# Dividing TensorE's step behind its sixth chunk in a one-core cached-attention kernel, with the maximum under a condition of its own

## The chip, the cores and the metric

The kernel runs on one core of a Trainium2 chip. The metric is the device time of one execution in microseconds (us). Three executions of the kernel before took 1268.61, 1270.12 and 1272.01 us; their median, 1270.12 us, is the time before. One more execution was profiled: 1268.6 us, of which the profile's span, from its first to its last instruction, is 1266.8 us.

## The reference

One token `x` of 448 numbers attends, with 16 query heads, to a cache of 8 key/value heads with 65,536 positions each, and the result is mixed with that of a small token mixer.

```python
q = (x @ wq)                                   # 16 heads of 256
k, v = repeat(k_cache, 2), repeat(v_cache, 2)  # each cached head serves 2 query heads
p = softmax(einsum("bhqd,bhkd->bhqk", q, k) * 256 ** -0.5)
a = einsum("bhqk,bhkd->bhqd", p, v).reshape(1, 1, 4096) @ wo
b = mixer(x)                                   # layernorm, 1792 features, gelu, back to 448
g = sigmoid((x * gate_w).sum(-1))
return g * a + (1 - g) * b
```

Keys and values are bf16, 268 MB each, and every one is used once.

## The kernel before, in words

The keys of the 8 heads are cut into `NP` = 32 *pairs* of 16,384 positions (4 to a head, `PPH`), numbered 0 to 31 here. A pair has `BODY` = 8 *chunks* of 2048 positions, 0 to 7. K and V of a pair are 8.4 MB each (`NV` = 128 rows of 64 KB).

**Transfers.** All large ones stand in SyncE's program, in one queue, in this order for pair j: K of pair j, when chunk 3 of pair j-1 has been transposed (`sem_tr`); then V of pair j-1, when the products of the probabilities and V of pair j-2 are done (`sem_pv`); with a head's first pair also its rows of `wo`, when the head before has been projected (`s_proj`). K lies in a ring of one and a half pairs (`kring`), V in one buffer (`vbuf`). The order was written out by hand; pairs 2, 3 and 31 have K in two halves. V of the last pair comes in five pieces (`pieces`): rows 0 to 47 go to the ring when pair 30 is transposed; 48 to 95, 96 to 111, 112 to 123 and 124 to 127 go to `vbuf` when the products of pair 30 are done (`sem_pv` at 31). Behind them come the two halves of the last head's `wo` (`sem_wl`).

**A chunk.** `transposes(k)` (L348) turns 16 tiles of 128x128 f32 words, four to each of four PSUM banks. VectorE (L681) copies two banks to SBUF and ScalarE (L821) the two others. `scores(k)` (L369) are 32 small matmuls against `qcur`, the two query columns of the head; they need the copies. Written T0 to T7 and S0 to S7 below.

**A pair's end.** `maxima` (L390, L392): VectorE reduces the scores to a running maximum per head (L687), TensorE transposes and spreads it, VectorE forms the negative maximum and the fading factor, ScalarE the exponentials `pT` (L808), and VectorE fades the accumulator `acc` (up to L710).

**Values.** `values(v)` adds pair v-1's part to `acc`: eight matmuls for the denominators (L397), then 128 matmuls with V's rows (L404); the wait for V stands between the two. For the last pair the first 48 rows are done in `first_of_last`, right behind the maximum, rows 48 to 111 in `values(32)`, and the last 16 in `tail` with the roles of the operands exchanged (L445), behind two matmuls that bring `acc` to the other layout (L452); then the last projection (L471) and the output.

**TensorE's loop** has 35 passes. Registers count the pairs: `k_reg` for `keys`, `l_reg` for `last_keys`, `v_reg` for `values`. In a steady pass it does, for pair j: `keys` (T0, then T1 S0 up to T6 S5), `values` of pair j-1, `last_keys` (T7 S6 S7), then, in a new head, the projection of the old one, for 14 pairs four matmuls of the mixer, then `maxima`. Of the first passes some hold only a part: `values` of pair 0 comes in a pass of its own before any keys of pair 1, and that of pair 1 before those of pair 2 (`cap_reg`, `LEAD` = 2). At the end, pass 33 holds `keys` of pair 31, `values` of pair 30, `last_keys` and `maxima` of pair 31 and `first_of_last`; pass 34 holds `values(32)` and `tail`. Before T0 of a head TensorE waits on `s_qc` for VectorE's copy of the head's queries to `qcur` (L767, behind the maximum, and where there is one the mixer step, of the head's last pair).

## Time and profile before

| what | us |
|---|---|
| three runs | 1268.61, 1270.12, 1272.01 |
| profiled execution | 1268.6 |
| its span | 1266.8 |
| TensorE matmuls busy | 922.7 |
| TensorE weight loads busy | 867.2 |
| ScalarE busy | 544.0 |
| VectorE busy | 497.1 |
| transposes L348, 4096 of them | 555.5 |
| values L404, 4032 of them | 122.1 |
| scores L369, 8192 of them | 236.7 |

The transfers move 544.22 MB in that span, 430 GB/s on average. Busy times of engines overlap each other, so they do not add up to the span; what matters is which engine or queue the others wait for at each place, and that is read from the chain of waits and the timeline.

### The profile page before, as it was taken

The numbers are of one execution on the slowest core, as the hardware profiler recorded it, in microseconds if no ns is written. First come the engines' busy times: TensorE is split into PE (matmuls) and PEld (weight loads), VectorE is DVE, ScalarE is ACT, GpSimd is POOL, SyncE is SP. The second block draws the span as 40 slices with busy tenths as digits, with TensorE's granted clock in tenths as the row PEclk, the third lists the DMA queues.
The fourth block names the chain that finished last, engine by engine and source line by source line (L and its number), as shares of the span: only waits on it lengthen the run. The fifth ranks groups of instructions, "written<-read, shape, count | busy, mean of one in ns | idle before, by whom it ended". The sixth has DMA issues, their size and how long they took to land.

```text
span 1266.8 us, 40261 instructions
## 1 busy us (share of the span) xinstructions
PE 922.7 (73%) x17201; PEld 867.2 (68%) x17201; DVE 497.1 (39%) x1125; ACT 544.0 (43%) x692; POOL 0.9 (0%) x7
## 2 busy tenths in 40 slices
PE   4588877678676687766887667876669766688685
PEld 3577866578676687665777566875668766687684
DVE  3233444343443444544445333333334332343341
ACT  2354543344433454443544334443444443354451
POOL 0000000000000000000000000000000000000000
PEclk9798887789777898778888789877789877898787
DMA  9999999999999999999999999999999999999998
GB/s 416 432 396 430 447 430 430 441 435 430 430 430 443 432 430 430 430 443 432 430 430 436 437 432 430 430 437 437 432 430 430 437 435 435 430 430 430 427 434 346
DMA packets 12054, 544.37 MB, mean 430 GB/s; under 512 B 1417, under 2 KB 1676, under 8 KB 2956
## 3 DMA queue, kind: packets, MB, share of 16 engines
q1 hardware_dynamic: 11954, 544.22, 99.6%
q8 instruction: 7, 0.11, 0.0%
q10 hardware_dynamic: 90, 0.01, 0.0%
q14 instruction: 3, 0.02, 0.0%
HBM read 544.22 MB, written 0.00 MB: 430 GB/s over the span
## 4 chain that ended last, share of the span: by engine, by line
DMA 68%; PE 30%; issue 1%; DVE 0%; SPq 0%; DVEq 0%
DMA kring<-in_A_k_cache_dram 65%; PE kst L348 24%; PE sps L369 5%; DMA vbuf<-in_A_v_cache_dram 3%; PE acc L404 2%; PE acc L397 0%; PE sps L392 0%; DVE mcol L687 0%; PE sps L445 0%; PE sps L452 0%; DVE acc L710 0%; PE sps L390 0%; DVE mrow L692 0%; DVE accs L715 0%; DVE mdiag L694 0%
## 5 line engine op out<-in xcount | busy, mean ns | idle before, releaser
L348 PE MATMUL kst<-ident,kring 128*128 128x128 f32 x4096 | 555.5, 296 | 266.8 <-DMA kring<-in_A_k_cache_dram 233.5
L821 ACT ACTIVATE ktT<-kst 128x1024 bf16<-128x1024 bf16 x512 | 498.5, 1021 | 539.9 <-PE kst L348 539.5
L348 PEld LDWEIGHTS kst<-ident,kring 128*128 128x128 f32 x4096 | 504.7, 154 | 281.3 <-issue 280.6
L681 DVE COPY ktT<-kst 128x1024 bf16<-128x1024 bf16 x512 | 354.2, 692 | 636.0 <-PE kst L348 612.1
L369 PEld LDWEIGHTS sps<-qcur,ktT 128*128 128x128 bf16 x8192 | 238.1, 96 | 2.6
L369 PE MATMUL sps<-qcur,ktT 128*128 128x2 bf16 x8192 | 236.7, 163 | 0.0
L404 PE MATMUL acc<-vbuf,pT 128*2 128x256 bf16 x4032 | 122.1, 282 | 5.9 <-DMA vbuf<-in_A_v_cache_dram 5.6
L404 PEld LDWEIGHTS acc<-vbuf,pT 128*2 128x2 bf16 x4032 | 94.3, 86 | 25.5 <-DMA vbuf<-in_A_v_cache_dram 5.7
L804 ACT ACTIVATE fade<-mdif 128x2 f32<-128x2 f32 x32 | 6.5, 203 | 112.0 <-DVE mdif L698 112.0
L392 PEld LDWEIGHTS sps<-mdiag,mones 2*128 2x128 f32 x64 | 13.0, 252 | 28.4 <-DVE mdiag L694 28.4
L392 PE MATMUL sps<-mdiag,mones 2*128 2x2 f32 x64 | 15.8, 313 | 21.3 <-DVE mdiag L694 21.3
L808 ACT ACTIVATE pT<-sps,mneg 128x64 f32 x128 | 30.4, 334 | 0.0
L826 ACT ACTIVATE z_b<-z_b 128x448 bf16<-128x448 bf16 x14 | 8.1, 576 | 48.1 <-DVE z_b L668 48.1
L687 DVE TENSOR_REDUCE mcol<-sps 128x2 f32<-128x256 f32 x32 | 13.5, 422 | 33.6 <-PE sps L369 33.6
L390 PE MATMUL sps<-ident,mcol 128*2 128x128 f32 x32 | 9.7, 302 | 12.9 <-DVE mcol L690 10.5
L397 PE MATMUL acc<-pT,ones_sq 128*128 128x32 bf16 x256 | 11.7, 179 | 7.7 <-DVE acc L710 3.4
L710 DVE TENSOR_SCALAR acc<-acc,fader 128x256 f32<-128x256 f32 x32 | 15.8, 493 | 2.5
L397 PEld LDWEIGHTS acc<-pT,ones_sq 128*128 128x128 bf16 x256 | 8.6, 97 | 10.8 <-issue 7.2
L692 DVE TENSOR_REDUCE mrow<-sps 2x1 f32<-2x128 f32 x32 | 8.9, 279 | 15.9 <-PE sps L390 15.9
L390 PEld LDWEIGHTS sps<-ident,mcol 128*2 128x2 f32 x32 | 2.6, 80 | 16.2 <-DVE mcol L690 12.6
L697 DVE TENSOR_SCALAR mneg<-sps 128x2 f32<-128x2 f32 x32 | 5.1, 159 | 18.7 <-PE sps L392 18.7
L460 PEld LDWEIGHTS acc<-sel,accs 128*64 128x64 f32 x112 | 10.8, 214 | 0.9
(108 smaller groups left out, 163.4 us busy)
## 6 DMA issues: line engine op xcount, KB each, us to landing
kring<-in_A_k_cache_dram SPq DMA_DIRECT2D x8, 4096.0 KB, 24.3
wo_sb<-in_A_wo_dram SPq DMA_DIRECT2D x7, 448.0 KB, 28.6
vbuf<-in_A_wq_dram SPq DMA_DIRECT2D x1, 3072.0 KB, 10.3
kring<-in_A_v_cache_dram SPq DMA_DIRECT2D x1, 3072.0 KB, 38.8
vbuf<-in_A_v_cache_dram SPq DMA_DIRECT2D x1, 3072.0 KB, 9.6
vbuf<-in_A_v_cache_dram SPq DMA_DIRECT2D x1, 1024.0 KB, 11.6
vbuf<-in_A_v_cache_dram SPq DMA_DIRECT2D x1, 768.0 KB, 13.1
vbuf<-in_A_wq_dram SPq DMA_DIRECT2D x1, 512.0 KB, 11.1
```

The source lines that it names most:

```text
L348: ins = pe.transpose(kst[:, b, i * P:(i + 1) * P], kring_f[:, at + NT * (k % DC) + 4 * b + i, :], ident[:, :])
L369: ins = pe.matmul(sps[:, 0, 2 * (NT * k + nt):2 * (NT * k + nt) + 2], ktT[:, par, b, ntl * DH + dj:(ntl + 1) * DH:2], qcur[:, dj, :], star ...
L390: pe.transpose(mxT, mcol[:, :], ident[:, :]).then_inc(s_mT, 1)
L392: pe.matmul(mxB, mones[:, :], mdiag[:, :], start=True, stop=True).then_inc(s_mB, 1)
L397: pe.matmul(acc[:, DENC:SELC], ones_sq[:, :], pT[:, r, :], start=False, stop=(r == BODY - 1), skip_group_check=True)
L404: ins = pe.matmul(acc[o:o + REP, 0:DH], pT[:, r, 2 * nt:2 * nt + 2], buf[:, n, :], start=False, stop=False, skip_group_check=True)
L460: ins = pe.matmul(dst[hh * HP:(hh + 1) * HP, i:i + 1], accs[:, i:DH:2 * REP], sel[:, hh:hh + 1], start=False, stop=True, skip_group_check= ...
L681: vec.tensor_copy(ktT[:, k % KTB, b, :], kst_b[:, b, :]).then_inc(sem_ev[b], 1)
L687: vec.tensor_reduce(out=mcol[:, :], in_=scores_all.rearrange("p (n hh) -> p hh n", hh=REP), axis=AX.X, op=ALU.max)
L710: vec.tensor_scalar(acc[:, 0:DENC], acc[:, 0:DENC], fader[:, :], None, op0=ALU.mult).then_inc(s_acc, 1)
L808: ins = act.activation(pT[:, bass.ds(p0, DC), hh:2 * NT:REP], scores_all.rearrange("p (a r n hh) -> p a hh r n", a=2, r=DC, hh=REP)[:, hal ...
L821: act.activation(ktT[:, k % KTB, b, :], kst_b[:, b, :], AF.Copy).then_inc(sem_ev[b], 1)
```

## The change

`keys` ends behind its sixth chunk, and `last_keys` takes the rest. A pair is then T0, T1 S0 up to T5 S4 | `values` of the pair before | T6 S5 T7 S6 S7 | maximum. A constant `CUT` = 6 says where.

`maxima`, with what stood ahead of it (projection, mixer matmuls) and `first_of_last` behind it, leaves the branch of `last_keys` and gets a branch of its own with a register of its own, `m_reg`: it runs when `last_keys` of that pair is done and `values` of all pairs before it (`v_reg == m_reg`).

`values` gets a second condition. `need_reg` is 0 until `keys` of pair 31 is done and 32 from then on, and `values` runs only if `l_reg >= need_reg`. So pass 33 holds `keys` and `last_keys` of pair 31 and nothing else, pass 34 `values` of pair 30, then the maximum of pair 31 and `first_of_last`, and a pass 35 is added with `values(32)` and `tail`.

The semaphore `s_qc`, TensorE's wait for it and the registers that counted heads for it go. `done` holds `c + 1` once for the four banks of a chunk. SyncE's, VectorE's and ScalarE's programs stay as they were but for the increments of `s_qc`.

```diff
+    CUT = 6
 ...
+                done = pe.snap(c + 1, min_val=1, max_val=NC)
 ...
-                        pe.wait_ge(sem_ev[b], c + 1)
+                        pe.wait_ge(sem_ev[b], done)
 ...
             def keys(c0, j, *where):
-                for k in range(1, BODY - 1):
+                for k in range(1, CUT):
                     transposes(k, c0 + k, j, *where)
                     scores(k - 1, c0 + k - 1, j1)
             def last_keys(c0, x2):
-                transposes(BODY - 1, c0 + (BODY - 1), None, None, x2)
-                for k in range(BODY - 2, BODY):
-                    scores(k, c0 + k, None)
+                for k in range(CUT, BODY):
+                    transposes(k, c0 + k, None, None, x2)
+                    scores(k - 1, c0 + k - 1, None)
+                scores(BODY - 1, c0 + BODY - 1, None)
 ...
-            with nc.Fori(0, NP + LEAD + 1, 1, engines=on, head_slot={pe.engine: 0}):
+            with nc.Fori(0, NP + LEAD + 2, 1, engines=on, head_slot={pe.engine: 0}):
                 with pe.If(val(k_reg) < val(cap_reg)):
-                    with pe.If(val(mk_reg) == PPH):
-                        pe.reg_mov(mk_reg, 0)
-                        pe.reg_add(gk_reg, gk_reg, 1)
-                    pe.wait_ge(s_qc, pe.snap(gk_reg, min_val=1, max_val=H))
                     keys(...)
-                    pe.reg_add(mk_reg, mk_reg, 1)
-                with pe.If(val(v_reg) < val(l_reg)):
-                    ... values(v) ...
+                    with pe.If(val(k_reg) == NP):
+                        pe.reg_mov(need_reg, NP)
+                with pe.If(val(v_reg) < val(m_reg)):
+                    with pe.If(val(l_reg) >= val(need_reg)):
+                        ... values(v) ...
                 with pe.If(val(l_reg) < val(k_reg)):
                     last_keys(...)
-                    ... projection of a head, mixer matmuls ...
                     pe.reg_add(l_reg, l_reg, 1)
-                    maxima(pe.snap(l_reg, min_val=1, max_val=NP))
-                    with pe.If(val(l_reg) == NP):
-                        first_of_last()
+                with pe.If(val(m_reg) < val(l_reg)):
+                    with pe.If(val(v_reg) == val(m_reg)):
+                        ... projection of a head, mixer matmuls ...
+                        pe.reg_add(m_reg, m_reg, 1)
+                        maxima(pe.snap(m_reg, min_val=1, max_val=NP))
+                        with pe.If(val(m_reg) == NP):
+                            first_of_last()
                 with pe.If(val(v_reg) == NP):
                     tail()
 ...
-            vec.tensor_copy(qcur[:, :, :], qT[:, :, 0:REP]).then_inc(s_qc, 1)
+            vec.tensor_copy(qcur[:, :, :], qT[:, :, 0:REP])
```

More of the change, by code (lines that the diff above doesn't have):

```diff
@@ L66, in bass_gated_mix__gqa_block_cached__mixer_token_mlp__decode_kernel @@
     NLATE = 112
+    CUT = 6
+    assert DC < CUT < BODY
     NRING = 48
@@ L198, in bass_gated_mix__gqa_block_cached__mixer_token_mlp__decode_kernel @@
         sem_kc = [new_sem("sem_kc%d" % i) for i in range(3)]
-        s_qc = new_sem("s_qc")
         sem_v = new_sem("sem_v")
@@ L530, in _ @@
             cap_reg = reg("cap_reg", 1)
-            mk_reg = reg("mk_reg", 0)
-            gk_reg = reg("gk_reg", 1)
+            m_reg = reg("m_reg", 0)
+            need_reg = reg("need_reg", 0)
             mv_reg = reg("mv_reg", 0)
@@ L551, in _ @@
                     pe.reg_add(k_reg, k_reg, 1)
-                    pe.reg_add(mk_reg, mk_reg, 1)
-                with pe.If(val(v_reg) < val(l_reg)):
-                    pe.reg_add(v_reg, v_reg, 1)
-                    pe.reg_add(mv_reg, mv_reg, 1)
-                    pe.reg_add(cap_reg, v_reg, 1)
-                    v = pe.snap(v_reg, min_val=1, max_val=NP)
-                    values(v)
-                    with pe.If(v >= LEAD):
-                        pe.reg_mov(cap_reg, NP)
+                    with pe.If(val(k_reg) == NP):
+                        pe.reg_mov(need_reg, NP)
+                with pe.If(val(v_reg) < val(m_reg)):
+                    with pe.If(val(l_reg) >= val(need_reg)):
+                        pe.reg_add(v_reg, v_reg, 1)
+                        pe.reg_add(mv_reg, mv_reg, 1)
+                        pe.reg_add(cap_reg, v_reg, 1)
+                        v = pe.snap(v_reg, min_val=1, max_val=NP)
+                        values(v)
+                        with pe.If(v >= LEAD):
+                            pe.reg_mov(cap_reg, NP)
                 with pe.If(val(l_reg) < val(k_reg)):
@@ L564, in _ @@
                     pe.reg_sub(x2l_reg, NV, x2l_reg)
-                    with pe.If(val(mv_reg) == PPH):
-                        pe.reg_mov(mv_reg, 0)
-                        g1 = pe.snap(gv_reg, min_val=1, max_val=H)
-                        pe.wait_ge(s_cp, g1)
-                        clear(acc[:, 0:NACC])
-                        by_row(acc[:, SELC:NACC]).then_inc(s_sel, 1)
-                        pe.wait_ge(sem_wo, pe.snap(g1 * 16, min_val=16, max_val=16 * H))
-                        pe.wait_ge(s_oTn, g1)
-                        project(range(2 * REP)).then_inc(s_proj, 1)
-                        pe.reg_add(gv_reg, gv_reg, 1)
@@ L575, in _ @@
-                    with pe.If(l > MIX0):
-                        with pe.If(l < MIX0 + FT + 1):
-                            pe.wait_ge(s_pb, val(mix_reg, 1, FT))
-                            pe.reg_add(mix_reg, mix_reg, 1)
-                            for q in range(NCG):
-                                pe.matmul(prj[32 * q:32 * q + 1, WG:2 * WG], w2cur[:, :],
-                                          gu[:, q * WG:(q + 1) * WG], start=False, stop=True, skip_group_check=True)
-                    pe.reg_add(l_reg, l_reg, 1)
@@ L583, in _ @@
-                    maxima(pe.snap(l_reg, min_val=1, max_val=NP))
-                    with pe.If(val(l_reg) == NP):
-                        first_of_last()
+                    pe.reg_add(l_reg, l_reg, 1)
+                with pe.If(val(m_reg) < val(l_reg)):
+                    with pe.If(val(v_reg) == val(m_reg)):
+                        with pe.If(val(mv_reg) == PPH):
+                            pe.reg_mov(mv_reg, 0)
+                            g1 = pe.snap(gv_reg, min_val=1, max_val=H)
+                            pe.wait_ge(s_cp, g1)
+                            clear(acc[:, 0:NACC])
+                            by_row(acc[:, SELC:NACC]).then_inc(s_sel, 1)
+                            pe.wait_ge(sem_wo, pe.snap(g1 * 16, min_val=16, max_val=16 * H))
+                            pe.wait_ge(s_oTn, g1)
+                            project(range(2 * REP)).then_inc(s_proj, 1)
+                            pe.reg_add(gv_reg, gv_reg, 1)
+                        with pe.If(val(m_reg) > MIX0):
+                            with pe.If(val(m_reg) < MIX0 + FT + 1):
+                                pe.wait_ge(s_pb, val(mix_reg, 1, FT))
+                                pe.reg_add(mix_reg, mix_reg, 1)
+                                for q in range(NCG):
+                                    pe.matmul(prj[32 * q:32 * q + 1, WG:2 * WG], w2cur[:, :],
+                                              gu[:, q * WG:(q + 1) * WG], start=False, stop=True, skip_group_check=True)
+                        pe.reg_add(m_reg, m_reg, 1)
+                        maxima(pe.snap(m_reg, min_val=1, max_val=NP))
+                        with pe.If(val(m_reg) == NP):
+                            first_of_last()
@@ L767, in _ @@
                     vec.tensor_copy(qcur[:, :, :], qT[:, :, bass.ds(vec.snap(q_reg, min_val=REP, max_val=HQ - REP), REP)]
-                                    ).then_inc(s_qc, 1)
+                                    )
                     vec.reg_add(q_reg, q_reg, REP)
```

## The prediction

> **What bounds the kernel now.** I read the page first, then the waits, then the end of the timeline with the transfers beside it, then the start. The page:

> ```profile
> span 1266.8 us, 40261 instructions
> ...
> DMA  9999999999999999999999999999999999999998
> ...
> DMA 68%; PE 30%; issue 1%; DVE 0%; SPq 0%; DVEq 0%
> ```

> The transfer engines are busy in every slice, and waiting for them makes up 68% of the chain. One pair (400.0 to 438.7 us, asked for as a stretch) moves 434 GB/s at a DMA share of 1.00. In the waits of the whole run

> ```profile
> PE kst L348 <- DMA kring<-in_A_k_cache_dram: 233.5, 29, 10.5
> ...
> PE acc L404 <- DMA vbuf<-in_A_v_cache_dram: 5.6, 1, 5.6
> ```

> TensorE waits for K 29 times, 233.5/29 = 8.1 us each, and for V once: for that of pair 30. So steady pairs are set by bytes; only places where the queue runs dry can pay. The timeline's end shows one:

> ```profile
> 1235.82 0.36 PE L397 MATMUL acc<-pT,ones_sq 128*128 128x32 bf16 x8
> 1241.79 6.09 PE L404 MATMUL acc<-vbuf,pT 128*2 128x256 bf16 x128 [5.61 <-DMA vbuf<-in_A_v_cache_dram]
> 1247.94 1.85 SPq L265 DMA_DIRECT2D vbuf<-in_A_v_cache_dram  x4
> 1247.96 1.96 PE L348 MATMUL kst<-ident,kring 128*128 128x128 f32 x16
> 1249.75 1.74 PE L369 MATMUL sps<-qcur,ktT 128*128 128x2 bf16 x64
> 1249.84 0.95 SPq L314 DMA_DIRECT2D wo_sb<-in_A_wo_dram  x2
> 1252.25 0.27 PE L390 MATMUL sps<-ident,mcol 128*2 128x128 f32 x1 [0.76 <-DVE mcol L690]
> 1256.46 2.73 PE L404 MATMUL acc<-kring,pT 128*2 128x256 bf16 x48
> 1259.79 2.23 PE L404 MATMUL acc<-vbuf,pT 128*2 128x256 bf16 x64 [0.27 <-issue]
> 1264.27 0.37 PE L471 MATMUL prj<-wo_sb,oTn 128*1 128x112 bf16 x16 [0.25 <-DVE oTn L728]
> ```

> The last V pieces are requested only when pair 30's values end (1247.9). The transfers by issue give 9.6, 11.6, 13.1 and 13.3 us to landing for the four and 13.4 for the last `wo` half: landings at 1257.5, about 1260.0, 1261.9, 1262.6 and 1263.7. The piece ahead of them (requested 1210.25, 38.8 us) landed at 1249.0, and the DMA share falls to 0.18 in 1247.5 to 1248.5 and 0.48 in 1249.5 to 1250.5: a hole of about 1.1 us, since a request takes about 1 us to its first packets.

> **Steady pairs: cost at nothing, by cover.** Work is moved, not added: T6 (1.81) and S5 (0.78), 2.6 us, go behind `values`. In pair 10 T6 began at 423.12, and V, requested at 389.70 with 34.7 us to landing, came at 424.4. The eight denominator matmuls and their branch (0.6) now come first, so TensorE waits some 0.7 us for V (in other pairs 0 to 2), a wait this trace lacks. Behind it stand the 128 matmuls (3.66), T6 S5, T7 at about 430.7 instead of 429.9, the maximum, ScalarE's and VectorE's copies, and T0. The cover is the wait for K before T0: 9.87 us here, 5.58 in the tightest steady pair (T0 at 365.36). Were it gone, K's request would be late, but that has a second cover: K is requested at 416.70, 7.7 us before V ahead of it lands. V's request (429.98 before) now goes 0.8 us later or up to 1.7 earlier, with K in transfer until 443.8. Bounds: 0 below, since no byte moves sooner; above, each us beyond 5.6 + 7.7 costs 28 us in all. I take 0.

> **The clock** could eat cover. Two neighbouring 3.41 us stretches (columns: length, busy PE, PEld, DVE, ACT, POOL, granted clock, DMA, GB/s):

> ```profile
> 1209.27:1212.68 3.41, 2.66 (x74) 2.51 (x72) 1.71 (x4) 1.94 (x2) 0.00 (x0) 1.00 0.92 396
> 1212.68:1216.09 3.41, 1.32 (x6) 1.09 (x6) 1.79 (x9) 1.06 (x5) 0.00 (x0) 0.50 0.99 423
> ```

> **The removed wait on `s_qc`: nothing.** The copy to `qcur` ended at 164.8, T0 of the next head began at 170.41, on K. S0 still follows VectorE's copy of chunk 0, which follows that copy. Register work, and the added branches of each pass, lie in the same cover.

> **The end: the gain.** SyncE's order, and when V of pair 30 lands (1241.75), stay. T6 S5 T7 S6 S7 of pair 31 took until 1235.7 + 1.8 + 1.6 = 1239.1 with nothing between; pair 30's late V (landing 1202.97 against T6's 1201.47) shifts all by about 0.9, to 1240.0; then branches and the way round the loop (1.4 between the last L392 at 131.2 and T0 at 132.65, an upper bound: behind 64 queued scores part of it hides) and denominators 0.4. That is 1240.4 to 1241.8: `values` starts about when it did. Its first wait for V still stands ahead of everything of the end.

> Behind `values` the maximum follows at once. L390 stood 1252.25 - 1247.88 = 4.4 us behind it; now about 0.5. With the same later steps the 48 ring rows end at 1259.19 - 3.9 = 1255.3 instead of 1259.2, and the next V piece lands at 1257.5: 2.2 of the 3.9 become a wait for it. From there landings rule: 16 rows behind 1260.0 end at 1260.7; copy and L452 (1.1) 1261.9; L445 behind 1262.6, ending 1262.9; the projection's second half behind 1263.7, ending about 1263.95 instead of 1264.67. **Gain 0.7 us** with the requests where they were.

> Requests can come sooner: TensorE was idle 5.61 us before `values`, ran it at half clock and needed 6.09; pair 10 needed 3.66. Now the idle time is about 2, with 1.6 of scores ahead of it: between cold and warm. If `values` ends 1 us sooner the hole of 1.1 us closes, and all landings with it: gain 1.8 and no more, as bytes then follow without a gap. I take 1.2, nearer neither end, since the phase of the 3.41 us stretches is not fixed by the kernel. Sum: 1266.8 - 1.2 = 1265.6 span, 1267.4 with the 1.8 us around it. The profiled execution is 1.5 under the median, so 1270.1 - 1.2 = **1268.9 us**.

> **Rival 1, warm: 1268.3.** [...] The mechanism from rows: `values` at 3.66 ends at 1245.5, requests 2.4 sooner, hole closed, gain 1.8. For: after 1.90 us of idling ahead of 72.56 the clock stayed at 1.00. Against: the two stretches above, which fell without an idle one. Chance 0.2.

> **Rival 2, slower: 1272.9.** TensorE's instructions arrive in packets, seven in all and none after 66 us. Twice the first pass waited for one; a packet at 50.7 and one at 58.3 stand before these rows (waits in brackets):

> ```profile
> 53.60 3.67 PE L348 MATMUL kst<-ident,kring 128*128 128x128 f32 x16 [9.51 <-issue]
> ...
> 61.26 0.37 PE L390 MATMUL sps<-ident,mcol 128*2 128x128 f32 x1 [2.30 <-issue]
> ```

> T7 and L390 each started 2.9 us behind their packet. The seventh started at 65.4, so what it holds runs from 68.3. [...] Then `values` of pair 0 starts at about 69 and, mostly at half clock, ends at 74.7 instead of 70.7; V of pair 1 (requested 70.71, when K had all but landed at 72.4) goes 4.0 later, the queue stands empty, and all behind moves: 1270.1 - 1.2 + 4.0. The moved T6 S5 themselves cost nothing there: they run from 46.6, in the gap of 9.51. [...] Chance 0.18. [...]

> **Rival 3, `values` late: 1271.4.** If shift, branches and a cold pair 30 (3.4) add up, `values` of pair 30 starts after V's landing; each us then opens the hole by one. Say 2 us late and at 6.09: landings 2.0 later, less the 0.7 gained, +1.3 net. For: little slack (0 to 1.3). Against: starting late, it starts warm. Chance 0.07.

> **Rival 4, it gains nothing: 1270.1.** The bytes end where they did and `wo` hides the rest. Chance 0.05; the forecast keeps 0.5.

> **Numbers.** 0.3%, 3.8 us, is about what a measurement of this kernel can tell from no change; no case alone reaches it. Low end: 1.8 gained and the runs' spread below the median, 1.5: 1266.8. High end: rival 2 and half a us: 1273.4. Faster by over 0.3%: 0.07, from rival 1 and spread. Slower: 0.11, rival 2 or 3 with spread, and cover I misjudged. Same: 0.82.

> **Right or wrong.** Right: waits for V before L408 (L404 so far) in most pairs, up to 2 us; K's landings 38.7 apart; L394 (L390 so far) within a us of the end of pair 30's values; DMA share near 1 from 1242 to the last landing; the wait for the next V piece behind the ring rows. Wrong: first V request of pair 1 after 72 us; T0 late for K in steady pairs; values of pair 30 starting after 1242.

## The result and the profile after

The changed kernel took **1275.17 us** (median of 9 runs, 1273.02 to 1276.88), the kernel before 1270.31 us in runs beside it (9 runs, 1267.86 to 1272.18). The ratio is 1.0038 with a 95% interval of 1.0026 to 1.0050: slower by 4.9 us. The forecast was 1268.9 us with a range up to 1273.4; the result lies above the range. Rival 2 is what happened, in the profiled run at a higher price than it was given, and the end gained nothing. The profiled execution took 1276.85 us, its span 1274.6 us.

From the page of the changed kernel:

```profile
DMA  9979999999999999999999999999999999999998
...
DMA 62%; PE 33%; issue 3%; DVE 1%; SPq 0%; DVEq 0%; ACT 0%
```

Before, all slices but the last of the DMA row were 9. Now the third one, 64 to 96 us, is a 7. The chain has 3% "issue" instead of 1%. The damage is done in one place near the start. The timeline there (start, duration, engine, line, idle time before), first before the change and then after it:

```profile
64.60 0.40 PE L397 MATMUL acc<-pT,ones_sq 128*128 128x32 bf16 x8 [1.72 <-DVE acc L710]
...
64.92 5.74 PE L404 MATMUL acc<-vbuf,pT 128*2 128x256 bf16 x128
70.71 0.33 SPq L265 DMA_DIRECT2D vbuf<-in_A_v_cache_dram  x1
```

```profile
63.54 0.37 PE L394 MATMUL sps<-ident,mcol 128*2 128x128 f32 x1 [3.06 <-issue]
...
71.50 0.40 PE L401 MATMUL acc<-pT,ones_sq 128*128 128x32 bf16 x8 [6.34 <-issue]
71.83 6.03 PE L408 MATMUL acc<-vbuf,pT 128*2 128x256 bf16 x128
77.91 0.33 SPq L266 DMA_DIRECT2D vbuf<-in_A_v_cache_dram  x1
```

The denominators of pair 0 waited 6.34 us for "issue", that is for nothing that the profile shows. VectorE's fading of `acc`, which they need, was done at 66.74. TensorE's seventh instruction packet (the times of packets are those of the records of TensorE's instruction queue) began at 67.76. V of pair 1 was requested at 77.91; before, at 70.71. K of pair 1 had landed at 72.58 and nothing else was in the queue. The stretches, with the columns of the prediction's clock rows:

```profile
70.00:72.00 2.00, 0.50 (x14) 0.40 (x18) 0.00 (x0) 0.00 (x0) 0.00 (x0) 0.50 0.01 4
72.00:74.00 2.00, 2.00 (x44) 1.32 (x40) 0.00 (x0) 0.00 (x0) 0.00 (x0) 0.50 0.00 0
...
78.00:80.00 2.00, 0.64 (x6) 0.64 (x7) 0.00 (x0) 0.00 (x0) 0.00 (x0) 1.00 1.57 524
```

From 70 on to behind 78 the queue moved next to nothing, for 8 us. V of pair 1 landed at 99.69 (before 92.67, so +7.02) and V of pair 30 at 1248.76 (before 1241.75, +7.01): what was lost at the start is carried through 29 pairs without a change. The end, from the timeline of TensorE and SyncE:

```profile
1242.19 1.96 PE L351 MATMUL kst<-ident,kring 128*128 128x128 f32 x16 [1.20 <-issue]
...
1246.57 1.74 PE L372 MATMUL sps<-qcur,ktT 128*128 128x2 bf16 x64
1250.77 0.38 PE L401 MATMUL acc<-pT,ones_sq 128*128 128x32 bf16 x8 [2.46 <-issue]
1251.08 5.22 PE L408 MATMUL acc<-vbuf,pT 128*2 128x256 bf16 x128
1256.35 1.80 SPq L266 DMA_DIRECT2D vbuf<-in_A_v_cache_dram  x4
1257.60 0.27 PE L394 MATMUL sps<-ident,mcol 128*2 128x128 f32 x1 [1.30 <-issue]
...
1266.01 1.48 PE L408 MATMUL acc<-vbuf,pT 128*2 128x256 bf16 x48 [0.74 <-DMA vbuf<-in_A_v_cache_dram]
1268.48 0.61 PE L408 MATMUL acc<-vbuf,pT 128*2 128x256 bf16 x16 [0.99 <-DMA vbuf<-in_A_v_cache_dram]
```

`values` of pair 30 no longer waits for V. It starts 2.3 us behind V's landing (1251.08 against 1248.76), so the last requests come 7.59 us behind that landing instead of 6.19, and the last landing is 23.32 us behind it instead of 21.95. From the last landing to the end it is 2.55 us instead of 3.10. Together, V of pair 30 to the end: 25.87 instead of 25.05, +0.82. So the profiled difference of 7.8 us is 7.0 at the start, nothing between and 0.8 at the end. The 0.8 alone shows little, since profiles with the same order of the end differ by more (below, under the end in the account of the prediction).

### The profile page after: what moved, and what is told of

The parts are those of the page before. It is cut to its first block, busy times and chain, and to the rows that moved or that the text cites. A ratio compares the mean times of both kernels' runs of the same rounds, so it can differ in the third digit from the quotient of the medians.

```text
span 1274.6 us, 40489 instructions
## 1 busy us (share of the span) xinstructions
PE 939.0 (74%) x17201; PEld 878.3 (69%) x17201; DVE 496.7 (39%) x1125; ACT 544.9 (43%) x692; POOL 0.9 (0%) x7
## 4 chain that ended last, share of the span: by engine, by line
DMA 62%; PE 33%; issue 3%; DVE 1%; SPq 0%; DVEq 0%; ACT 0%
DMA kring<-in_A_k_cache_dram 47%; PE kst L351 23%; DMA vbuf<-in_A_v_cache_dram 14%; PE sps L372 6%; PE acc L408 3%; DMA wo_sb<-in_A_wo_dram 1%; PE sps L396 0%; PE acc L401 0%; DVE mcol L692 0%; SPq L266 0%; PE sps L394 0%; PE acc L464 0%; DVE mrow L697 0%; DVE mdiag L699 0%; DVE acc L715 0%
## 5 line engine op out<-in xcount | busy, mean ns | idle before, releaser
L351 PE MATMUL kst<-ident,kring 128*128 128x128 f32 x4096 | 562.6, 299 | 201.1 <-DMA kring<-in_A_k_cache_dram 164.5
L351 PEld LDWEIGHTS kst<-ident,kring 128*128 128x128 f32 x4096 | 511.1, 155 | 215.6 <-issue 213.5
L408 PE MATMUL acc<-vbuf,pT 128*2 128x256 bf16 x4032 | 128.1, 290 | 16.8 <-DMA vbuf<-in_A_v_cache_dram 16.6
L408 PEld LDWEIGHTS acc<-vbuf,pT 128*2 128x2 bf16 x4032 | 97.8, 89 | 40.3 <-DMA vbuf<-in_A_v_cache_dram 17.2
L394 PE MATMUL sps<-ident,mcol 128*2 128x128 f32 x32 | 10.0, 311 | 22.4 <-DVE mcol L695 16.9
L394 PEld LDWEIGHTS sps<-ident,mcol 128*2 128x2 f32 x32 | 2.6, 80 | 25.8 <-DVE mcol L695 20.0
L585 PE MATMUL prj<-gu,w2cur 128*1 128x112 bf16 x56 | 3.3, 222 | 15.8 <-issue 15.8
## 6 DMA issues: line engine op xcount, KB each, us to landing
vbuf<-in_A_wq_dram SPq DMA_DIRECT2D x1, 3072.0 KB, 10.5
```

What stands on the lines that cost most here:

```text
L351: ins = pe.transpose(kst[:, b, i * P:(i + 1) * P], kring_f[:, at + NT * (k % DC) + 4 * b + i, :], ident[:, :])
L394: pe.transpose(mxT, mcol[:, :], ident[:, :]).then_inc(s_mT, 1)
L408: ins = pe.matmul(acc[o:o + REP, 0:DH], pT[:, r, 2 * nt:2 * nt + 2], buf[:, n, :], start=False, stop=False, skip_group_check=True)
```

## The experiments

**Theory A:** the branch back to the loop's top (entry 1817 of the list that TensorE's program builds to before the change, 1823 after it) now lies in the seventh instruction packet, so `values` of pair 0 and with it V of pair 1 wait for that packet, and the queue runs dry. **Theory B:** the loss comes from what the change moves or adds (T6 S5, the added branches, the order of pair 31). The spans and medians of the first four runs stand beside a kernel before of 1268.88 us (16 runs).

**The branch alone moved.** The kernel before with four tiny matmuls (eight instructions) in front of `tail`, where they run once, in the last pass. They push the branch back from entry 1817 to 1825; steady passes run what they ran.

```diff
             def tail():
+                for _ in range(4):
+                    pe.matmul(kst[:, 0, 0:2], ones_sq[0:1, :], zrow[0:1, 0:2], ...)
                 pe.wait_ge(s_cp, H)
```

> The kernel before with four tiny matmuls (eight instructions) more at the head of tail, so that nothing moves but the branch back to the loop's top: entry 1825 of TensorE's list instead of 1817. Theory A (the branch lies in the last code packet): the values of pair 0 wait for the seventh packet, start near 69 instead of 64.6 us, V of pair 1 is requested near 75 instead of 70.7, and the run is 3 to 5 us longer than the kernel before. Theory B (the loss comes from the moved chunk, the separate condition or the end): the same time as the kernel before, within 1 us.

Measured: 1275.06 us median, ratio 1.0051 [1.0037, 1.0064]; profiled 1271.39, span 1269.6. From its timeline:

```profile
60.85 0.27 PE L390 MATMUL sps<-ident,mcol 128*2 128x128 f32 x1 [1.85 <-issue]
...
69.07 0.40 PE L397 MATMUL acc<-pT,ones_sq 128*128 128x32 bf16 x8 [6.71 <-issue]
69.40 4.80 PE L404 MATMUL acc<-vbuf,pT 128*2 128x256 bf16 x128
74.25 0.33 SPq L265 DMA_DIRECT2D vbuf<-in_A_v_cache_dram  x1
```

The wait of 6.71 us for issue is there, with none of the change's work in the kernel. V of pair 1 landed at 96.14 and V of pair 30 at 1245.01, 3.5 and 3.3 us later than before. The median lies further off than the profiled run, which is the fastest of the five (up to 1276.89); the table below shows one cause that may be behind such a spread.

**The branch alone moved back.** The changed kernel with `tail` behind the loop, so that the branch back is entry 1719.

```diff
-                with pe.If(val(v_reg) == NP):
-                    tail()
+            tail()
```

> The changed kernel with tail written behind the loop instead of in it, so that the branch back is entry 1719 instead of 1823; order of work unchanged. Theory A: the values of pair 0 no longer wait for the seventh packet, V of pair 1 is requested near 73 instead of 77.9 us (the code packets may stay 2.3 us later than before), and the run is 4 to 5 us shorter than the changed kernel, within 2 us of the kernel before. Theory B: as long as the changed kernel, 1275 us.

Measured: 1269.13 us, ratio 1.0007 [0.9997, 1.0018]; profiled 1267.41, span 1265.6. Its start and its end:

```profile
64.16 0.39 PE L401 MATMUL acc<-pT,ones_sq 128*128 128x32 bf16 x8 [1.72 <-DVE acc L714]
64.48 5.30 PE L408 MATMUL acc<-vbuf,pT 128*2 128x256 bf16 x128
69.83 0.33 SPq L266 DMA_DIRECT2D vbuf<-in_A_v_cache_dram  x1
```

```profile
1241.61 0.36 PE L401 MATMUL acc<-pT,ones_sq 128*128 128x32 bf16 x8 [1.93 <-issue]
...
1248.53 0.27 PE L394 MATMUL sps<-ident,mcol 128*2 128x128 f32 x1 [1.30 <-issue]
```

The denominators wait for VectorE again, as before the change, and the whole loss is gone, with all of the change's work still there. The two runs together settle theory A against B for the start.

**The division alone.** The kernel before with the step divided behind chunk 6 and nothing else; the branch back stays at entry 1817.

```diff
-                for k in range(1, BODY - 1):
+                for k in range(1, 6):
...
```

> The kernel before with the step divided behind the sixth chunk and nothing else: the branch back stays entry 1817, the end keeps its order, so T6 S5 T7 S6 S7 stand between the values of pair 30 and the last maximum. Theory A: V of pair 1 requested near 71 to 73 us, run 0 to 3 us longer than the kernel before (the last maximum starts 2.6 us later, of which landings hide a part). Theory B, with the moved chunk as the cause: 4 to 5 us longer.

Measured: 1272.32 us, ratio 1.0029 [1.0017, 1.0041]; profiled 1272.94, span 1271.1: 3.4 us above the kernel before, where 0 to 3 was expected. V of pair 1 was requested at 72.33, with no wait for the seventh packet, and V of pair 30 landed 1.4 us later than before (the table below says why). The larger loss lies at the end: T6 S5 of pair 31 now stand behind `values` of pair 30.

```profile
1243.15 5.97 PE L405 MATMUL acc<-vbuf,pT 128*2 128x256 bf16 x128 [7.92 <-DMA vbuf<-in_A_v_cache_dram]
1249.19 1.96 PE L348 MATMUL kst<-ident,kring 128*128 128x128 f32 x16
...
1256.07 0.27 PE L391 MATMUL sps<-ident,mcol 128*2 128x128 f32 x1 [0.75 <-DVE mcol L691]
```

The maximum comes 12.96 us behind V of pair 30 (1243.11) instead of 10.50, and from that landing to the end it is 28.03 us instead of 25.05. So the division makes the end 3.0 us worse unless pair 31 is taken ahead, as the change does.

**The rest without the division.** The changed kernel with `CUT = 7`; the branch back stays at entry 1823.

```diff
-    CUT = 6
+    CUT = 7
```

> The changed kernel with the step divided where it was before, behind the seventh chunk (CUT = 7); the branch back stays entry 1823. Theory A: V of pair 1 requested 4 us or more later than before, run 3 to 5 us longer than the kernel before. Theory B, with the moved chunk as the cause: the same as the kernel before; with the end as the cause: 4 to 5 us longer with the request of V of pair 1 near 71 us.

Measured: 1273.74 us, ratio 1.0047 [1.0033, 1.0061]; profiled 1271.58, span 1269.8. Denominators of pair 0 at 68.98, V of pair 1 requested at 74.21, landed at 96.25: late, with T6 S5 where they were before. V of pair 30 to the end: 24.75.

**Filling the empty stretch.** SyncE's order at the start, in the changed kernel and in the one before: the lower half of K of pair 2 (chunks 4 to 7) is requested ahead of V of pair 1, and V of pair 2 between the two halves of K of pair 3.

```diff
+                    load_v(j - 1)                     # V of pair 2, behind the first half of K of pair 3
...
-                    load(kring, A_k_cache, j, 0, HV, 0, sem_kc[0])
...
+                if j == LEAD - 1:
+                    eng.wait_ge(sem_tr[NB - 1], BODY * (LEAD - 1))
+                    load(kring, A_k_cache, LEAD, 0, HV, 0, sem_kc[0])
...
-                elif j > LEAD:
+                elif j > LEAD + 1:
```

The changed kernel with it:

> Changed kernel; SyncE requests the lower half of K of pair 2 (4.2 MB, 9.7 us at 434 GB/s) at the start, when chunk 7 of pair 0 is transposed, ahead of V of pair 1; V of pair 2 moves to between the two halves of K of pair 3. Theory A (the loss is the queue that runs dry from 70 to 79 us because the branch back waits for the seventh instruction packet): the branch is as late as before (denominators of pair 0 at 69 to 71.5, V of pair 1 requested at 74 to 78), but the queue is full meanwhile, the DMA share stays near 1 from 70 to 82, and the time falls by some 5 to 8 us under the changed kernel's, to 1267 to 1270. Theory B (the loss lies in the moved chunk, the branches or the end): the time stays at 1273 to 1276.

The kernel before with it:

> Kernel before with the same new order of SyncE's requests at the start. Theory A: only its own small hole before 72 us (about 0.9 us) is closed, so 0.5 to 2 us shorter than before, 1267 to 1269; it and the changed kernel with the same edit then lie within 1.5 us of each other. Theory B: the kernel before gains as little, but the changed one stays 4 to 6 us behind it.

Measured (kernel before beside them 1270.13 us, 8 runs): 1283.74 us, ratio 1.0110 [1.0094, 1.0125], and 1281.19 us, ratio 1.0087 [1.0073, 1.0101]. Both expectations of the time failed, because of my edit. The stretch at 70 us was filled: the DMA share is 0.93 from 72 to 76 and 1.18 from 76 to 80 in the first. But V of pair 2 now went out ahead of the last half of K of pair 3, and behind that half nothing could be requested until chunk 3 of pair 3 was transposed. Stretches of the kernel before with the edit:

```profile
148.00:152.00 4.00, 1.89 (x9) 1.90 (x10) 0.68 (x1) 0.00 (x0) 0.00 (x0) 0.50 0.10 41
152.00:156.00 4.00, 4.00 (x25) 4.00 (x24) 1.61 (x4) 2.64 (x3) 0.00 (x0) 0.62 0.00 0
156.00:160.00 4.00, 4.00 (x88) 3.98 (x87) 1.86 (x3) 3.29 (x4) 0.00 (x0) 1.00 0.00 0
```

The hole was moved from 70 us to 149 us and made longer, since K then waits for the transposes with no V in transfer beside them. One thing these two still show: the denominators of pair 0 were at 69.03 in the first and 64.35 in the second, and V of pair 1 was requested at 74.97 and 70.81, yet it landed at 101.29 and 101.51, ahead of the new hole. With other work in the queue, the late branch cost nothing up to there. That is theory A's second half: the harm is the empty queue and not TensorE's wait.

**Sooner requests at the end,** on top of that edit: V rows 48 to 111 of pair 31 requested when row 112 of pair 30's values is done (`s_early`) and not at their end.

```diff
                 elif n0 == NRING:
+                    eng.wait_ge(s_early, NP - 1)
+                elif n0 == NLATE:
                     eng.wait_ge(sem_pv, NP - 1)
```

> Kernel before with the new order at the start, and the two last V pieces of rows 48 to 111 requested when row 112 of pair 30's values is done and not at its end. If the hole of about 1.1 us at 1247.5 to 1250.5 is worth its length, as the prediction's sum has it, requests 0.7 us sooner bring 0.5 to 0.8 us more: 1266.3 to 1268.3. If wo and the last projection hide it, nothing.

> Changed kernel with both edits of SyncE's order. If the end of the changed kernel is held by the late start of pair 30's values (2.3 us behind V's landing), the sooner requests bring 0.5 to 0.8 us over the same kernel without them: 1266.5 to 1269. If the earlier maximum is worth something once the requests come sooner, this one is ahead of the kernel before with both edits by up to 0.6 us; if the late start eats it, level or up to 1.5 us behind.

Measured: 1281.42 us, ratio 1.0097 [1.0082, 1.0112], and 1282.38 us, ratio 1.0098 [1.0084, 1.0112]. V of pair 30 to the end: 25.21 (25.87 without the sooner requests) in the kernel before, 25.12 (27.14) in the changed one, where the matmuls with V of pair 30 began 3.7 us behind its landing without them and 2.1 with them. The first of these requests went out 0.4 us ahead of the end of `values`, and not the 0.7 expected. The expected times, 1266.3 to 1269, were missed with the start's edit in the kernel. The gain itself is inconclusive: the medians move by +0.2 and -1.4 and the intervals overlap.

The same edit without the start's:

> Kernel before, only the end's requests moved: V rows 48 to 111 of pair 31 requested when row 112 of pair 30's values is done. If bytes hold the end, the hole in the queue at 1247.5 to 1250.5 shrinks by 0.6 to 0.8 us and the time by as much: 0.5 to 1 us under the kernel before (ratio 0.9992 to 0.9996), landing of V of pair 30 to the end 24.2 to 24.6 us instead of 25.05. If wo and the projection hide it: 25.0 and no difference.

And on the changed kernel with `tail` behind the loop:

> Changed kernel with tail behind the loop (its branch back in the sixth packet again) and the same sooner requests. Theory A for the start: V of pair 1 requested at 69.5 to 73 as in the run with tail behind the loop, not at 77.9. End: from V of pair 30's landing to the end 24.87 us there; with the requests some 0.7 us sooner 24.1 to 24.4, so 0.5 to 1 us under the kernel before and level with the kernel before with the same edit to within 0.6 us: what the earlier maximum gains is then real but small. If the late start of pair 30's values (0.9 us behind its landing) holds the end, 24.9 and nothing gained.

Measured, beside a kernel before of 1269.77 us (21 runs): 1268.92 us, ratio 0.9995 [0.9986, 1.0004], and 1269.34 us, ratio 0.9997 [0.9988, 1.0007]. V of pair 30 to the end: 24.83 and 24.38. Neither can be told from the kernel before; no version that is measurably faster was found. Of the expected lengths the second was hit (24.1 to 24.4), the first missed by 0.2.

All twelve profiles sort into four groups by two facts: the packet that holds the branch back, and when TensorE's third packet began (36.3 to 36.9, or 38.7 to 38.8; nothing in between):

| branch back in | third packet | seventh packet began | denominators of pair 0 | V of pair 1 requested |
|---|---|---|---|---|
| sixth (entries 1719, 1817) | early, 5 profiles | 65.2 to 65.4 | 64.16 to 64.60 | 69.83 to 70.81 |
| sixth | late, 2 | 67.8, 67.9 | 66.71, 66.74 | 72.16, 72.33 |
| seventh (1823, 1825) | early, 3 | 65.1 to 65.3 | 68.98 to 69.07 | 74.21 to 74.97 |
| seventh | late, 2 | 67.6, 67.8 | 71.50, 71.58 | 76.86, 77.91 |

Behind the branch the denominators start 3.7 to 4.0 us after the seventh packet's beginning, in all five. On average the branch costs them 4.7 to 4.8 us whether packets are early or late; late packets alone cost them 2.4. In V of pair 1's landing (profiles with SyncE's old order) the four groups stand at 92.0 to 92.7, 94.1 to 94.2, 96.1 to 96.3, and 99.7, in each of these eight profiles 21.8 to 22.2 us behind V's request.

## Why the prediction was wrong, by its steps

**The step that failed: the start taken as unchanged.** The sum, 1270.1 - 1.2, has no term for the start; the profiles show 3.5 to 7.0 us lost there, by the landing of V of pair 1. The prediction described the right mechanism in rival 2 (`values` of pair 0 held until the seventh packet, V's request 4.0 us later, the queue empty) but gave it 0.18. That chance was the author's estimate: no row of before shows at which entry the seventh packet begins, and no run shows how many entries a packet holds. The runs bound the edge: 1817 lies in the sixth packet, 1823 in the seventh, so it is at one of 1818 to 1823. The times of rival 2 were right: `values` of pair 0, for which it had "about 69", came at 68.98 to 69.07, and V's request, for which its sum gives 74.7, at 74.2 to 75.0, where the packets were early.

**Its price held for early packets and was too low for late ones.** Rival 2 had 4.0 less 1.2, thus 1272.9, and the range ended half a us above it. With early packets V of pair 1 landed 3.5 us later (two profiles); in the profiled run of the changed kernel it was 7.0. I took the packet times of one profile as fixed. In that run the third packet and all behind it were also 2.3 us late, and the denominators came 6.9 later: 2.1 as in the two profiles with late packets and the branch in the sixth, and the branch's 4.8. The rest is the length of `values` of pair 0, behind which V is requested. It took 5.74 us before, 4.80 and 4.86 with early packets behind the branch, which hid 0.9 of the branch's cost, and 6.03 in the changed kernel, which hid nothing and added 0.3. The granted clock goes with it: from 72 to 74 us it was 1.00 in the padded kernel and 0.50 in the changed one. Over runs, start and end together cost the 4.9 us of the medians. What share of the unprofiled runs had late packets is not recorded.

**The end: 1.2 gained in the sum, 0.8 lost in the trace.** Three terms were off. The sum had T6 to S7 of pair 31 with nothing between, done at 1240.0 and so 1.75 us ahead of V's landing; TensorE stood idle for 1.20 us ahead of T6, and the chunks ended at 1248.31, only 0.45 ahead of it. The way round the loop was bounded at 1.4 from one row; it took 2.46 in the changed kernel, 2.38 with `CUT = 7`, and 1.93 and 1.95 with `tail` behind the loop, where one branch less stands in the way. By the source the passes of the change run more branches than the one that gave that row, so it was no bound. Together this put `values` 2.3 us behind V: rival 3's mechanism, which had a chance of 0.07 and 2 us. The maximum came 1.30 behind `values` and not 0.5. `values` itself took 5.22 us for 6.09 before, about the 1 us less that the sum had between cold and warm.

The gain behind the last landing was 0.55 for 0.7 predicted, and that step held: all six profiles with the change's order of the end have 2.55 or 2.56 us there, the five with the order of before 2.98 to 3.51. It was eaten by requests 1.4 us later, where the sum counted on half a us from sooner ones. The 0.8 as a whole is not beyond chance: from V of pair 30's landing to the end, the order of before took 24.58 to 25.87 us in three profiles (24.58 in the padded kernel), and the order of the change 24.75 to 27.14 in four. With all repaired as far as I tried (sooner requests, shorter way round) the end is 24.38 us, which no comparison here can tell from these.

**Rival 1, the clock.** TensorE was idle for 2.46 us at most ahead of `values` of pair 30, with scores before it:

```profile
1250.00:1252.00 2.00, 1.23 (x28) 0.73 0.97 418
1252.00:1254.00 2.00, 2.00 (x44) 0.50 1.00 430
```

(Columns: length, busy PE, granted clock, DMA share, GB/s.) The clock halved all the same, near 1250.9 by the 0.73 of the first row, and the 3.41 us ahead of that hold 0.8 us of scores. In the clock records of both traces every stretch but the one at the end of the record lasts a whole multiple of 3.41 us. Cut at these places into pieces of 3.41 us, the kernel before has 239 at full clock; the next piece is at half clock behind 31 of them, which hold a median of 0.84 us of matmuls other than scores, and at full clock behind 208, which hold 2.28. The two groups overlap (up to 2.46, and from 1.22), so that scores count for little is an estimate that fits these numbers, and no run here tests it.

**What was right.** Steady pairs cost nothing: from V of pair 1's landing to that of pair 30 it is 1149.08 us before and 1149.07 after. Waits for V appeared as said, hidden under the wait for K; from the waits of the changed kernel:

```profile
PE kst L351 <- DMA kring<-in_A_k_cache_dram: 164.5, 28, 7.9
...
PE acc L408 <- DMA vbuf<-in_A_v_cache_dram: 16.6, 22, 1.4
```

V is waited for 22 times, in 20 pairs of the loop up to 1.4 us (0 to 2 predicted) and twice at the end, and the wait for K fell from 233.5 to 164.5 in all without running out. The wait behind the ring rows was there (0.74). Of the prediction's signs of being right, two failed: the maximum stood 1.30 behind `values`, and the DMA share fell to 0.35 in 1254 to 1256. Of its signs of being wrong two came, V of pair 1 requested behind 72 us and `values` of pair 30 behind V.

In the changed kernel's span TensorE's instruction queue, q8, whose packets are 16 KB each, has

```profile
q8 instruction: 7, 0.11, 0.0%
```

that is seven packets, the last at 67.76, in 36 passes with many branches each. No packet came in the passes behind it, so only the first way through the code waited for one.

## What to carry to other kernels

Before a change that adds instructions to a loop, look where its branch back and its first-pass blocks lie against the instruction packets, and what request waits behind them; a few entries that run once can cost some 5 us (3 to 6 here), and moving a piece of code that runs once behind the loop gives it back (medians of 1275.17 and 1269.13 us here). If one request alone keeps a queue busy, anything in front of that request is on the critical path, even in a kernel that waits for bytes everywhere else; other work in the queue hides it (V landed at 101.29 and 101.51 here, with 4.2 us between the requests), but what is taken ahead must not leave a hole at its old place; the one filling tried here did, and cost more than it saved. A bound for control flow taken from one row holds for the branches of that row only.

## What the hardware showed that I had not expected

Instruction packets have a place in time of their own. While K and V fill the queue, TensorE's packets from the third to the seventh begin 6.7 to 7.6 us apart in all twelve profiles, and the third begins early or 2.3 us late by what looks like chance: the same choice came out both ways in kernels with the same code ahead of it (36.30 and 38.81 in the two changed kernels with the start's edit). What sets it is open, and so is what part it has in the spread of 4 us from run to run.
